# Weight sums of the first Strassen pair: read from the slots where they are made, or through DRAM

## The chip, the cores and the metric

One core of a Trainium2 chip. The metric is the device time of the kernel in microseconds (us), the median of three runs; a profile of one more execution stands beside it. Engines: PE (TensorE, matmuls), ACT (ScalarE), DVE (VectorE), POOL (GpSimd); all DMAs of the work spoken of here are issued by SP (SyncE), in order.

## The reference

Banded attention feeds a gated feed-forward layer; everything is float32.

```python
scores = scale * np.matmul(q, k.transpose(0, 1, 3, 2))      # 8 x 8 heads, 576 x 64 each
scores = np.where((rel >= 0) & (rel < 64), scores, -1000000000.0)
scores = scores - np.max(scores, axis=-1, keepdims=True)
attn = np.exp(scores)
attn = attn / (np.sum(attn, axis=-1, keepdims=True) + 1e-09)
out = np.matmul(attn, v)
...
x = np.ascontiguousarray(attn_out.transpose(0, 2, 1, 3)).reshape(B * S, H * D)   # 4608 x 512
gate = 1.0 / (1.0 + np.exp(-(x @ w_gate)))                   # 512 -> 1536
val = x @ w_val
return (gate * val @ w_out).astype(np.float32)               # 1536 -> 512
```

The weights arrive as 64-bit numbers and are brought to float32 on the chip.

## The kernel before

**Tiles.** The 4608 tokens are worked through in 12 tiles of 384. Attention of a tile gives x, transposed (`xf`); the feed-forward layer takes it up to 1536 hidden rows, in 12 blocks of 128, for the gate and for the value (m = 0, 1), and down again. A float32 matmul is done as three, with each operand split in a rounded part and the rest (`split`, L144: a CAST on ACT, L145, and a subtraction, L146).

**Strassen pairs.** Tiles 0 and 1 go up with plain products (L342). The ten others go up in five pairs, s = 1 to 5. For a pair, a block k (0 to 5) and an m, the blocks k and k + 6 for both tiles are made by seven products (`product`, L519, matmuls in L537, six of 128x384 each) in place of eight. Their weight sides are called A11, S2, S1, S3, A12, A22 and S4. The A parts are blocks of the weights; the S parts are sums and differences of these. A product's partial results are gathered in three PSUM banks per pair (pr0, pr1, pr2), with only one buffer each, and combined by DVE (u and c, L543). The first product of an m uses pr0 and so waits for all readers of pr0 of the m before; the fourth uses pr1 and waits for DVE's u.

**Where the weight parts lie.** All 14 parts of a k lie in DRAM, in seven tiles `wd[k][q]` of two parts (512 KB). The A parts are put there when the weights are converted (L140). The S parts are made once, for twelve (m, k): `sums_load` (L453) brings two float32 blocks back, `sums_make` (L464) makes four sums on POOL, `sums_split` (L474) splits them (CAST on ACT, subtraction on POOL) into two tiles `ws`, and `sums_store` (L482) writes these to `wd` in four DMAs. For each pair `w_load` (L440) loads the seven tiles of a k. The tiles `ws` and the loaded tiles `wt` take turns in one ring of seven slots (tag "W", WB = 7).

**Order.** A list of events with a planned time each (`put`) is sorted and gives the order in which instructions are handed to a scheduler; the engines run in that order. Into the pairs' stages are laid the pieces of attention for the pair after (scores and softmax L208, L230, L239; transposes L283, L288; outputs L312 with their copies `xf` on ACT, L267 to L271; normalise L249 to L252) and the down products (L407). In the stage s = 1 POOL has only the sums and their splits to do: normalise (L252) and the sums of x run on DVE there.

Of the kernel before, what the change touches and what calls it, by code (L numbers as in the profile page):

```python
# [9 lines left out]
F32 = mybir.dt.float32  # L10
F32R = mybir.dt.float32r
# [7 lines left out]
P = 128  # L19
# [7 lines left out]
def attn_ffn(ctx: ExitStack, tc: tile.TileContext, qT, kT, vN, w_gate, w_val, w_out, out):  # L27


    nc = tc.nc  # L30
    NTOK, DM = out.shape
# [11 lines left out]
    RAW, W32 = 6, 3  # L43

    const = ctx.enter_context(tc.tile_pool(name="const", bufs=1))
    wts = ctx.enter_context(tc.tile_pool(name="wts", bufs=1))
    xp = ctx.enter_context(tc.tile_pool(name="xp", bufs=1))
    mp = ctx.enter_context(tc.tile_pool(name="mp", bufs=2))
# [10 lines left out]
    for key in ((0, 0), (1, 0), (0, 1)):  # L59
        m = const.tile([P, P], F32, name=f"m_{key[0]}{key[1]}")  # L60
# [65 lines left out]
    def conv_c(i):  # L126
        j, m = divmod(i, KINDS)
        _, w32 = conv.pop(i)
        H = DM // 2
        tag, bufs = ("W", WB) if m < 2 else (f"wo_{j}", 1)  # L130
        w2 = wts.tile([P, 2, 2, H], F32R, name=f"w{m}_{j}", tag=tag, bufs=bufs)
        if m == 2:
# [19 lines left out]
    WB = 7  # L152
# [245 lines left out]
    def down(t, j, i, first, last):  # L398
# [9 lines left out]
        if last:  # L408
# [11 lines left out]
            else:  # L420
# [10 lines left out]
    PRODUCTS = [("A11", "B11", 0), ("S2", "T2", 1), ("S1", "T1", 2), ("S3", "T3", 1),  # L431
                ("A12", "B21", 0), ("A22", "T4", 1), ("S4", "B22", 2)]
    NPR = len(PRODUCTS)
    wd = [[dr.tile([P, 2, 2, DM // 2], F32, name=f"wd_{k}_{q}") for q in range(NPR)] for k in range(NK)]
    wt = {}
# [2 lines left out]
    hb = {}  # L438

    def w_load(s, k, q):  # L440
        wt[(s, k, q)] = wts.tile([P, 2, 2, DM // 2], F32R, name=f"wt_{s}_{k}_{q}", tag="W", bufs=WB)
        nc.sync.dma_start(out=wt[(s, k, q)].bitcast(F32), in_=wd[k][q])

    def put_part(m, k, name, parts):
        n = [w for w, _, _ in PRODUCTS].index(name)
# [1 line left out]
        nc.sync.dma_start(out=wd[k][q][:, half], in_=parts.bitcast(F32))  # L447


    EARLY = {(0, 0): 8, (1, 0): 10, (0, 1): 12, (1, 1): 8}  # L450
    sums = {}

    def sums_load(m, k):  # L453
        aa = []
        for i in range(2):
            if (m, k) in EARLY:
                a = xp.tile([P, DM], F32, name=f"a{i}_{m}_{k}", tag=f"x{EARLY[m, k] + i}")
            else:
                a = mp.tile([P, DM], F32, name=f"a{i}_{m}_{k}", tag="w32", bufs=W32)
            nc.sync.dma_start(out=a, in_=w32d[m][k + i * NK])  # L460
            aa.append(a)
        sums[m, k] = aa
# [9 lines left out]
        sums[m, k] = sw  # L472

    def sums_split(m, k):  # L474
        H = DM // 2
        sw, sums[m, k] = sums[m, k], []
        for i in range(0, 4, 2):
            w2 = wts.tile([P, 2, 2, H], F32R, name=f"ws{i}_{m}_{k}", tag="W", bufs=WB)
            split(sw[:, i:i + 2, :], w2[:, :, 0, :], w2[:, :, 1, :], nc.gpsimd)
            sums[m, k].append(w2)  # L480

    def sums_store(m, k):  # L482
        for i, w2 in enumerate(sums.pop((m, k))):
# [35 lines left out]
    def product(s, k, m, n):  # L519
        _, x, b = PRODUCTS[n]  # L520
        new = n in (0, 1, 2)
        if new:
            bk = psum(s, b, f"pr{b}_{m}_{s}_{k}")
            tmp[b] = bk[:, :TT]
            if n == 0:
                tmp["first"] = bk
        ps = tmp[b]
        q, half = divmod(NPR * m + n, 2)
        w2 = wt[(s, k, q)]
        prs = []  # L530
        for c in range(2):
            cs = slice(c * P, (c + 1) * P)
            whi, wlo = w2[:, half, 0, cs], w2[:, half, 1, cs]
            x2 = xs[(s, x, c)]
            prs += [(whi, x2[:, 0, :]), (whi, x2[:, 1, :]), (wlo, x2[:, 0, :])]
        for i, (l, r) in enumerate(prs):
            pe(nc.tensor.matmul(ps, l, r, start=new and i == 0, stop=i == len(prs) - 1,  # L537
                                skip_group_check=not new))
        nm = f"{m}_{s}_{k}"

        def plus(a, tag):
            o = mp.tile([P, TT], F32, name=f"{tag}{n}_{nm}", tag=tag, bufs=2)
            nc.vector.tensor_add(out=o, in0=ps, in1=a)  # L543
            return o

        if n == 0:
            tmp["p1"] = mp.tile([P, TT], F32, name=f"p1_{nm}", tag="p1", bufs=1)
            nc.scalar.copy(tmp["p1"], ps)  # L548
        elif n == 1:
            tmp["u2"] = plus(tmp["p1"], "u")  # L550
        elif n == 3:
            u3 = plus(tmp["p1"], "u")
            ps = tmp[2]
            result(s, k, m, 1, 1, plus(u3, "c"))
        elif n == 4:
            result(s, k, m, 0, 0, ps)
        elif n == 5:
            result(s, k, m, 1, 0, plus(tmp["p1"], "c"))
        elif n == 6:
            result(s, k, m, 0, 1, plus(tmp["u2"], "c"))  # L560
# [29 lines left out]
    def put(tm, o, f, *a):  # L590
        events.append((tm, o, f, a))
# [35 lines left out]
    at, now = {}, 0.0  # L627
# [14 lines left out]
    for i, (kind, t, j) in enumerate(plan):  # L642
        attend(i)
        at[(kind, t, j)] = now
        if (kind, t, j) == ("up", 0, 0):
            now = -9
# [12 lines left out]
        if (kind, t, j) == ("up", 0, 0):  # L659
            now = 0.0  # L660
    for i in range(KINDS * NF):
        j, m = divmod(i, KINDS)
# [29 lines left out]
    for s in range(1, NS):  # L692
        a, b = 2 * s, 2 * s + 1
        for c in range(2):
            put(now - 21 + 10 * c, 5, x_parts, s, c)
            for n in range(NPR):
                put(now - 19.5 + 10 * c + 1.2 * n, 5.5, x_part, s, n, c)
                put(now - 18 + 10 * c + 1.2 * n, 5.6, x_rest, s, n, c)
        downs = []
        fill.clear()  # L700
        if s + 1 < NS:

            for n, (i, d) in enumerate(((2, 7), (12, 9), (26, 5), (33, 9), (47, 5), (54, 9), (68, 5), (75, 5))):
                fill[i] = [(3, *unit(s + 1, n), *([unit(s + 1, n - 1)] if n else []))]
                fill[i + (2 if n else 4)] = [(4, *unit(s + 1, n))]
                fill[i + d] = [(1, *unit(s + 1, n))]
            fill[82] = [(2, *unit(s + 1, n))]
        slot = 0
        for k in range(NK):
            if s == 1:  # L710
                for m in range(2):
                    for d, f in ((-8, sums_load), (0, sums_make), (8, sums_split), (12, sums_store)):
                        put(now - 50 + 12 * m + d, 7, f, m, k)
            for q in range(NPR):
                put(now - (12 if s == 1 else 24) + 3 * q, 7.5, w_load, s, k, q)
            for m in range(2):
                for n in range(NPR):
                    put(now, 9, product, s, k, m, n)
                    now += PRT
                    if n in (2, 4, 6) and len(downs) > (RESERVE if m else 0) * (k == 1):  # L720
                        j, x = downs.pop(0)
                        put(now, 9, down, a, j, x, j == 0, False)
                        now += DPT
                    attend(slot)
                    slot += 1
            downs += [(j, x) for j in (k, k + NK) for x in range(TB)]
        for j, x in downs:
            put(now, 9, down, a, j, x, False, j == NF - 1)
            now += DPT
        last_tile(b, [n // 2 + (n % 2) * NK for n in range(NF)],  # L730
                        (4, lambda t, j, s=s: hidden_b(s, j)))
    events.sort(key=lambda x: (x[0], x[1]))
    for _, _, f, a in events:
        if f in (conv_a, conv_b, conv_c):
            with ExitStack() as behind:
                j, m = divmod(a[0], KINDS)
# [54 lines left out]
```

## Time and profile before

| | |
|---|---|
| median of three runs | 1011.78 us (1010.85 to 1012.56) |
| profiled execution, its own time | 1013.32 us |
| its span, first to last instruction | 1011.5 us |
| busy: PE, DVE, ACT, POOL | 97%, 67%, 52%, 23% |
| stage of pair s = 1 | 218.75 to 389.46 us |
| stages of s = 2 and s = 3 | 389.46 to 549.70, 549.70 to 710 us |
| loads wt<-wd, stores wd<-ws in all | 210 of 512 KB, 48 of 256 KB |

The span is shorter than the execution's own time by what lies before the first and behind the last instruction. A busy share is an average over all stages; what a single stage costs is read from windows and timelines of that stage. A timeline row gives start, duration, engine, line and tiles; a bracket behind it gives the idle time of the engine before it and what ended that.

### The profile page before, as it was taken

The page shows a single profiled execution, that of the slowest core. Times are in us where ns is not written, and L with a number is a line of the kernel's source. Part 1 is how long each engine was busy: PE and PEld are TensorE (multiplying, and loading weights), DVE is VectorE, ACT ScalarE, POOL GpSimd, SP SyncE. Part 2 cuts the span into 40 slices and gives each one's busy share as a digit, 9 for nine tenths or more (in the row PEclk, how much of TensorE's full clock was granted, in tenths as well). Part 3 has the DMA queues.
Part 4 walks back from the last instruction along what each step waited for, and adds up shares of the span by engine and source line. Part 5 has one row for each costly group of instructions (what it writes and reads, how often), then busy time and mean ns, then how long its engine had stood idle before and what let it go on. Part 6 is the DMA issues. An engine that isn't in the chain of part 4 may idle for free.

```text
span 1011.5 us, 19901 instructions
## 1 busy us (share of the span) xinstructions
PE 981.8 (97%) x6984; PEld 884.0 (87%) x6984; DVE 675.8 (67%) x1846; ACT 527.2 (52%) x1465; POOL 236.1 (23%) x251
## 2 busy tenths in 40 slices
PE   5899999998999999999999999999999999999998
PEld 4798998887899978999988999988999998999996
DVE  6789889757887874766675766675666677344542
ACT  7878886744654644545554654554555454211122
POOL 5200117254540030212131221213211124010100
PEclk9999999999999999999999999999999999999999
DMA  9899988899997624767652776760776662466500
GB/s 299 297 348 367 342 288 278 277 333 342 320 324 267 216 85 152 232 220 221 202 172 70 240 234 200 222 204 32 228 232 219 207 192 74 146 219 204 192 32 32
DMA packets 115924, 221.52 MB, mean 219 GB/s; under 512 B 9456, under 2 KB 61936, under 8 KB 115824
## 3 DMA queue, kind: packets, MB, share of 16 engines
q1 hardware_dynamic: 115824, 220.24, 65.9%
q8 instruction: 56, 0.92, 0.4%
q14 instruction: 44, 0.36, 0.1%
HBM read 178.52 MB, written 41.68 MB: 218 GB/s over the span
## 4 chain that ended last, share of the span: by engine, by line
PE 73%; DVE 7%; ACT 7%; DMA 6%; issue 3%; POOL 1%; SPq 0%; DVEq 0%; ACTq 0%; POOLq 0%
PE pr L537 36%; PE y L407 24%; PE ph L342 6%; ACT p L239 3%; PE pp L283 2%; PE s L208 2%; DMA wd<-w 2%; DMA wd<-ws 2%; ACT g L352 1%; ACT e L351 1%; PE oo L312 1%; PE s L312 1%; DMA wt<-wd 1%; DVE u L543 1%; DVE p L230 1%
## 5 line engine op out<-in xcount | busy, mean ns | idle before, releaser
L537 PE MATMUL pr<-x_T,wt 128*128 128x384 f32 x1440 | 284.6, 339 | 4.7 <-DVE u L543 3.6
L537 PEld LDWEIGHTS pr<-x_T,wt 128*128 128x128 f32 x1440 | 252.6, 188 | 20.1 <-DVE u L543 11.2
L407 PE MATMUL y<-w,hh 128*128 128x512 f32 x804 | 250.2, 392 | 0.0
L537 PE MATMUL pr<-x_B,wt 128*128 128x384 f32 x1080 | 222.2, 342 | 4.7 <-ACT xf L267 4.0
L537 PEld LDWEIGHTS pr<-x_B,wt 128*128 128x128 f32 x1080 | 188.7, 189 | 15.6 <-ACT xf L267 4.3
L407 PEld LDWEIGHTS y<-w,hh 128*128 128x128 f32 x804 | 148.3, 188 | 21.3 <-ACT hh L372 1.3
L543 DVE TENSOR_TENSOR u<-pr,p 128x384 f32<-128x384 f32 x120 | 66.6, 555 | 143.3 <-PE pr L537 143.0
L407 PE MATMUL y<-w,hl 128*128 128x512 f32 x402 | 158.6, 394 | 0.5 <-DVE hl L376 0.4
L252 POOL TENSOR_TENSOR p<-p,rs 128x384 f32<-128x384 f32 x76 | 65.0, 860 | 278.2 <-DVE rs L250 227.5
L239 ACT ACTIVATE p<-p,mn 128x128 f32<-128x128 f32 x288 | 111.1, 394 | 23.6 <-DVE mn L230 22.7
L376 POOL TENSOR_TENSOR hl<-h,hh 128x384 fp32r<-128x384 f32 x48 | 49.8, 1038 | 296.2 <-DVE hh L374 296.2
L342 PE MATMUL ph<-x,w 128*128 128x384 f32 x576 | 109.2, 343 | 1.8 <-DVE w L146 1.3
L342 PEld LDWEIGHTS ph<-x,w 128*128 128x128 f32 x576 | 100.9, 190 | 5.4 <-DVE w L146 1.6
L407 PEld LDWEIGHTS y<-w,hl 128*128 128x128 f32 x402 | 75.3, 187 | 19.3 <-DVE hl L376 3.1
L230 DVE CUSTOM_DVE_ANT_0 p<-s,m 128x128 f32<-128x128 f32 x288 | 66.4, 285 | 15.7 <-PE s L208 8.5
L543 DVE TENSOR_TENSOR c<-pr,u 128x384 f32<-128x384 f32 x120 | 66.6, 555 | 7.8 <-ACT g L568 3.3
L376 DVE TENSOR_TENSOR hl<-hb,hh 128x384 fp32r<-128x384 f32 x60 | 39.1, 663 | 40.9 <-ACT hh L372 40.5
L351 ACT ACTIVATE e<-c 128x384 f32<-128x384 f32 x72 | 37.4, 522 | 52.6 <-DVE c L543 51.6
L548 ACT COPY p<-pr 128x384 f32<-128x384 f32 x60 | 28.2, 470 | 70.4 <-PE pr L537 69.8
L288 ACT COPY pT<-pp 128x384 f32<-128x384 f32 x96 | 41.2, 481 | 41.6 <-PE pp L283 41.6
L356 DVE SCALAR_TENSOR_TENSOR g<-g,e 128x384 f32<-128x384 f32 x96 | 55.2, 589 | 5.7 <-ACT e L353 5.6
L354 DVE TENSOR_SCALAR g<-g 128x384 int32<-128x384 int32 x96 | 40.2, 425 | 25.9 <-ACT g L352 25.9
(84 smaller groups left out, 1238.7 us busy)
## 6 DMA issues: line engine op xcount, KB each, us to landing
wt<-wd SPq DMA_DIRECT2D x210, 512.0 KB, 4.2
v<-in_vN_dram SPq DMA_DIRECT2D x48, 384.0 KB, 4.9
wd<-ws SPq DMA_DIRECT2D x48, 256.0 KB, 5.3
k<-in_kT_dram SPq DMA_DIRECT2D x48, 224.0 KB, 5.0
q<-in_qT_dram SPq DMA_DIRECT2D x48, 192.0 KB, 4.7
wd<-w SPq DMA_DIRECT2D x36, 256.0 KB, 6.0
out_dram<-yo SPq DMA_DIRECT2D x33, 256.0 KB, 2.0
raw<-in_moe_w_gate_dram SPq DMA_DIRECT2D x12, 512.0 KB, 5.9
```

The costliest lines, as they stand in the source:

```text
L230: nc.vector.tensor_tensor_reduce(out=pt[:, u, :], in0=sc[:, u, :], in1=masks[key], op0=ALU.add, op1=ALU.min, scale=-SCALE, scalar=3.0e38, ...
L239: exp = nc.scalar.activation(pt[:, u, :], pt[:, u, :], AF.Exp, bias=mn[:, u:u + 1], scale=-1.0, **sums)
L252: eng.tensor_mul(out=pt, in0=pt, in1=rs.unsqueeze(2).broadcast_to([P, UP, P]))
L288: cp = nc.scalar.copy(pT, pp)
L342: pe(nc.tensor.matmul(ph, l, r, start=i == 0, stop=i == len(prs) - 1))
L351: nc.scalar.activation(e, ph, AF.Relu, scale=-1.0)
L354: nc.vector.tensor_scalar(out=g.bitcast(I32), in0=g.bitcast(I32), scalar1=0x7FFFFFFF, scalar2=None, op0=ALU.bitwise_and)
L356: nc.vector.scalar_tensor_tensor(out=g, in0=g, scalar=1.0, in1=e, op0=ALU.add, op1=ALU.mult)
L376: return eng.tensor_sub(out=h_lo, in0=h32, in1=h_hi.bitcast(F32))
L407: pe(nc.tensor.matmul(yb[y], l, r, start=first and n == 0, stop=last and n == 2))
L537: pe(nc.tensor.matmul(ps, l, r, start=new and i == 0, stop=i == len(prs) - 1, skip_group_check=not new))
L543: nc.vector.tensor_add(out=o, in0=ps, in1=a)
```

## The change

For the first pair, the products read the S parts from the tiles `ws` in which they were made; only the six A parts of a k are loaded (`a_load`: three tiles `wa`, two DMAs of 256 KB each). The stores stay, since the pairs after read all parts from DRAM. `wt` is now kept by part. The planned times of the sums are set anew: the sums of all k but 0 are made 21 before the k's first product, in place of 50, with a step of 13 between the two m, in place of 12, and of k = 0 by 38 before it. Two of the early sums get other tiles.

```diff
     def w_load(s, k, q):
-        wt[(s, k, q)] = wts.tile([P, 2, 2, DM // 2], F32R, name=f"wt_{s}_{k}_{q}", tag="W", bufs=WB)
-        nc.sync.dma_start(out=wt[(s, k, q)].bitcast(F32), in_=wd[k][q])
+        w2 = wts.tile([P, 2, 2, DM // 2], F32R, name=f"wt_{s}_{k}_{q}", tag="W", bufs=WB)
+        nc.sync.dma_start(out=w2.bitcast(F32), in_=wd[k][q])
+        for half in range(2):
+            wt[(s, k, *divmod(2 * q + half, NPR))] = w2[:, half]
+
+
+    OTHERS = [((0, 0), (0, 4)), ((0, 5), (1, 0)), ((1, 4), (1, 5))]
+
+    def a_load(s, k, x):
+        w2 = wts.tile([P, 2, 2, DM // 2], F32R, name=f"wa_{k}_{x}", tag="W", bufs=WB)
+        for i, (m, n) in enumerate(OTHERS[x]):
+            q, half = divmod(NPR * m + n, 2)
+            nc.sync.dma_start(out=w2[:, i].bitcast(F32), in_=wd[k][q][:, half])
+            wt[(s, k, m, n)] = w2[:, i]
...
-    EARLY = {(0, 0): 8, (1, 0): 10, (0, 1): 12, (1, 1): 8}
+    EARLY = {(0, 0): 8, (1, 0): 10}
...
+            elif (m, k) == (0, 1):
+                if i == 0:
+                    both = mp.tile([P, 2, DM], F32, name=f"a_{m}_{k}", tag="raw", bufs=RAW)
+                a = both[:, i, :]
...
             sums[m, k].append(w2)
+            for e in range(2):
+                n = [w for w, _, _ in PRODUCTS].index(f"S{i + e + 1}")
+                wt[(1, k, m, n)] = w2[:, e]
...
-        q, half = divmod(NPR * m + n, 2)
-        w2 = wt[(s, k, q)]
+        w2 = wt[(s, k, m, n)]
...
-            whi, wlo = w2[:, half, 0, cs], w2[:, half, 1, cs]
+            whi, wlo = w2[:, 0, cs], w2[:, 1, cs]
...
-                    for d, f in ((-8, sums_load), (0, sums_make), (8, sums_split), (12, sums_store)):
-                        put(now - 50 + 12 * m + d, 7, f, m, k)
-            for q in range(NPR):
-                put(now - (12 if s == 1 else 24) + 3 * q, 7.5, w_load, s, k, q)
+                    for d, f in ((-6, sums_load), (0, sums_make), (7, sums_split), (11, sums_store)):
+                        put(now - (21 if k else 38) + 13 * m + d, 7, f, m, k)
+                for x, d in enumerate((-18, -14, -5)):
+                    put(now + d, 7.5, a_load, s, k, x)
+            else:
+                for q in range(NPR):
+                    put(now - 24 + 3 * q, 7.5, w_load, s, k, q)
```

The change alters the order on ACT, SP and POOL. On ACT, at the end of the first k and the start of the second of s = 1, before the change (ws0_0_3 is the first tile of sums of m = 0, k = 3, xf_4_0 a piece of x of tile 4, p0_4_2 a piece of its softmax, pr0_1_1_0 the bank pr0 for m = 1, s = 1, k = 0):

```order
L353 ACTIVATE e_3_0_3243<-e_3_0_3243 128x384
L288 COPY pT0_4_0_3301<-pp0_4_0_3297 128x128
L288 COPY pT1_4_0_3307<-pp1_4_0_3303 128x128
L145 CAST ws0_0_3_3403<-sw_0_3_3255 128x2x256
L145 CAST ws2_0_3_3406<-sw_0_3_3255 128x2x256
L267 COPY xf_4_0_3369<-pr0_1_1_0_3266 128x128
L268 COPY xf_4_0_3369<-s1_4_2_3356 128x128
L239 ACTIVATE p0_4_2_3384,rs0_4_2_3386<-p0_4_2_3384,mn0_4_2_3385 128x128 x3
L271 COPY xf_4_0_3369<-s0_4_2_3355 128x128
L239 ACTIVATE p1_4_2_3394,rs1_4_2_3396<-p1_4_2_3394,mn1_4_2_3395 128x128 x3
L548 COPY p1_0_1_1_3427<-pr0_0_1_1_3420 128x384
```

The same place of ACT after the change:

```order
L353 ACTIVATE e_3_0_3183<-e_3_0_3183 128x384
L288 COPY pT0_4_0_3244<-pp0_4_0_3240 128x128
L288 COPY pT1_4_0_3250<-pp1_4_0_3246 128x128
L145 CAST ws0_1_1_3355<-sw_1_1_3224 128x2x256
L267 COPY xf_4_0_3307<-pr0_1_1_0_3206 128x128
L268 COPY xf_4_0_3307<-s1_4_2_3294 128x128
L239 ACTIVATE p0_4_2_3322,rs0_4_2_3324<-p0_4_2_3322,mn0_4_2_3323 128x128 x3
L271 COPY xf_4_0_3307<-s0_4_2_3293 128x128
L145 CAST ws2_1_1_3358<-sw_1_1_3224 128x2x256
L239 ACTIVATE p1_4_2_3332,rs1_4_2_3334<-p1_4_2_3332,mn1_4_2_3333 128x128 x3
L567 COPY p1_0_1_1_3368<-pr0_0_1_1_3361 128x384
L145 CAST ws0_0_2_3433<-sw_0_2_3341 128x2x256
```

Before, both CASTs of the sums of m = 0, k = 3 stood ahead of the first xf copy, three k ahead of their use. Now one CAST of m = 1, k = 1 stands there, the second behind the xf copies, and the first of m = 0, k = 2 ahead of the gate activations of k = 1.

On SP, around the start of the stage, before the change (yo are output rows, a0 and a1 the two blocks of `sums_load`, wt the loads of weight parts):

```order
L422 DMA out_0_dram<-yo_1_0_3077 128x512
L442 DMA wt_1_0_6_3209<-wd_0_6_168 128x1024
L422 DMA out_0_dram<-yo_1_1_3091 128x512
L422 DMA out_0_dram<-yo_1_2_3102 128x512
L442 DMA wt_1_1_0_3211<-wd_1_0_169 128x1024
L460 DMA a0_0_3_3125<-w32d_0_3_140 128x512
L167 DMA q_4_2_3249<-in_qT_dram 128x384
L460 DMA a1_0_3_3127<-w32d_0_9_146 128x512
L168 DMA k_4_2_3250<-in_kT_dram 128x448
```

SP around the same place after the change (wa are the loads of `a_load`):

```order
L422 DMA out_0_dram<-yo_1_0_3026 128x512
L422 DMA out_0_dram<-yo_1_1_3043 128x512
L476 DMA a0_1_1_3123<-w32d_1_1_150 128x512
L422 DMA out_0_dram<-yo_1_2_3054 128x512
L476 DMA a1_1_1_3125<-w32d_1_7_156 128x512
L476 DMA a0_0_2_3229<-w32d_0_2_139 128x512
L453 DMA wa_1_0_3066<-wd_1_0_169 128x512
L453 DMA wa_1_0_3066<-wd_1_2_171 128x512
L167 DMA q_4_2_3190<-in_qT_dram 128x384
L168 DMA k_4_2_3191<-in_kT_dram 128x448
```

The blocks for the sums of m = 1, k = 1 are now loaded between and behind the output stores of tile 1, where before the blocks of m = 0, k = 3 were; the loads of weight parts are half as large.

## Rows read from the trace of the kernel before

**Rows 1.** The page's span and busy time of each engine.

```profile
span 1011.5 us, 19901 instructions
PE 981.8 (97%) x6984; PEld 884.0 (87%) x6984; DVE 675.8 (67%) x1846; ACT 527.2 (52%) x1465; POOL 236.1 (23%) x251
```

**Rows 2.** Windows: us, busy PE, PEld, DVE, ACT, POOL; PE clock, DMA share, GB/s.

```profile
218.75:300.00 81.25, 73.70 (x570) 67.50 (x569) 63.16 (x170) 44.11 (x136) 38.21 (x39) 0.98 0.96 330
240.00:260.00 20.00, 17.90 (x93) 17.36 (x93) 13.20 (x37) 11.08 (x34) 6.90 (x7) 0.91 0.91 332
...
218.75:389.46 170.71, 162.62 (x1154) 145.15 (x1153) 124.45 (x326) 88.88 (x265) 49.31 (x48) 0.99 0.74 250
389.46:549.70 160.24, 159.61 (x1153) 143.92 (x1153) 105.32 (x298) 81.97 (x250) 35.15 (x36) 1.00 0.59 189
```

**Rows 3.** Timeline of PE, 218 to 300 us.

```profile
219.82 2.24 PE L537 MATMUL pr<-x_T,wt 128*128 128x384 f32 x12
...
227.84 1.33 PE L537 MATMUL pr<-x_B,wt 128*128 128x384 f32 x6 [0.57 <-ACT g L352]
...
242.10 2.29 PE L537 MATMUL pr<-x_B,wt 128*128 128x384 f32 x6 [4.03 <-ACT xf L267]
244.18 2.80 PE L537 MATMUL pr<-x_T,wt 128*128 128x384 f32 x12
...
248.58 1.20 PE L537 MATMUL pr<-x_B,wt 128*128 128x384 f32 x6
...
253.12 1.23 PE L537 MATMUL pr<-x_B,wt 128*128 128x384 f32 x6
...
266.02 1.31 PE L537 MATMUL pr<-x_T,wt 128*128 128x384 f32 x6 [0.81 <-DVE c L543]
...
269.69 1.32 PE L537 MATMUL pr<-x_T,wt 128*128 128x384 f32 x6 [1.66 <-DVE u L543]
...
282.14 1.31 PE L537 MATMUL pr<-x_T,wt 128*128 128x384 f32 x6 [0.23 <-DVE u L543]
...
292.75 1.32 PE L537 MATMUL pr<-x_T,wt 128*128 128x384 f32 x6 [0.25 <-DVE u L543]
```

**Rows 4.** Timeline of ACT, 241 to 265 us.

```profile
241.26 0.62 ACT L145 CAST ws<-sw 128x512 fp32r<-128x512 f32 x1 [6.54 <-DMA wd<-ws]
241.78 0.26 ACT L267 COPY xf<-pr 128x128 f32<-128x128 f32 x1
...
263.96 0.62 ACT L145 CAST ws<-sw 128x512 fp32r<-128x512 f32 x1 [2.59 <-DMA wd<-ws]
```

**Rows 5.** The chain that ended last, 218 to 300 us: start, us, what.

```profile
234.86 6.30 DMA wd<-ws
```

**Rows 6.** Timeline of DVE, 266 to 270 us.

```profile
266.69 1.67 DVE L252 TENSOR_TENSOR p<-p,rs 128x384 f32<-128x384 f32 x1
...
269.09 0.54 DVE L543 TENSOR_TENSOR u<-pr,p 128x384 f32<-128x384 f32 x1
```

**Rows 7.** Timeline of POOL, 257 to 267 us.

```profile
257.63 1.06 POOL L468 TENSOR_TENSOR sw<-a 128x256 f32<-128x256 f32 x1
258.66 0.73 POOL L470 TENSOR_TENSOR sw<-a,a 128x256 f32<-128x256 f32 x1
...
266.65 1.29 POOL L146 TENSOR_TENSOR ws<-sw,ws 128x512 fp32r<-128x512 f32 x1 [0.71 <-ACT ws L145]
```

**Rows 8.** By line (ns min/median/max): L252 to 300 us, L252 after, L352 in both.

```profile
L252 DVE TENSOR_TENSOR p<-p,rs x8: 548/558/1674, 225.5 to 280.8; 128x384 f32<-128x384 f32 x8
...
L252 DVE TENSOR_TENSOR p<-p,rs x6: 549/550/560, 301.5 to 336.7; 128x384 f32<-128x384 f32 x6
...
L352 ACT ACTIVATE g<-c x18: 507/518/527, 226.5 to 348.0; 128x384 f32<-128x384 f32 x18
```

**Rows 9.** DMA issues 218 to 345 us (KB, us to landing); SP's waits, 150 to 400.

```profile
wt<-wd SPq DMA_DIRECT2D x40, 512.0 KB, 5.4
...
SPq L442 <- PE pr L537: 47.0, 28, 3.1
```

## The prediction

> **What bounds the kernel now.** The page is read first: TensorE (PE) is busy for 981.8 of a span of 1011.5 us, 97% [rows 1], so a change can give back only time in which PE waits or runs slowly, and the question is whether such time lies in the stage that the change touches. The busy time by windows answers it. A stage of a Strassen pair that has nothing to do with the weight sums, the second, lasts 160.24 us, and PE works for 159.61 of them. The first pair's stage, which makes the sums, lasts 170.71 us, with PE busy for 162.62 [rows 2]. So the first pair costs 10.5 us more than its successor, of which 8.1 us is idle and the rest is slower matmuls. Those 10.5 us are the most that this change can give.
>
> The timeline of PE then shows where they lie [rows 3]. Idle: 0.57 us before 227.84, behind ScalarE's (ACT's) gate activation; 4.03 us before 242.10, behind ACT's copy xf; 0.81 us before 266.02, behind a VectorE (DVE) addition c; 1.66, 0.23 and 0.25 us before 269.69, 282.14 and 292.75, behind DVE's u. Slow: the six matmuls at 242.10 take 2.29 us where six at 227.84 take 1.33, and the twelve at 244.18 take 2.80 where twelve at 219.82 take 2.24, which makes 0.96 + 0.56 = 1.52 us. The granted clock of 240 to 260 is 0.91 of full, a spell at 1.2 GHz within a stretch at 2.4, where other rows have about 1 [rows 2]; before it fell PE had been idle for the 4.03 us. So the slow matmuls are a second bill for the same wait.
>
> What ended the 4.03 us is read on ACT [rows 4]: a CAST of a weight sum (L145) stood at the head of ACT's queue for 6.54 us and was let go by a DMA wd<-ws, a store; the xf copy for which PE waited came right behind it, at 241.78. The chain shows that store as its longest piece there, 6.30 us from 234.86 [rows 5]. The CAST needs one of the seven W slots, and the slot is free only when the sum that lay in it has been written out to DRAM. The 0.81 us has the same source one step later: another CAST waited 2.59 us for such a store until 263.96 [rows 4], the score copies behind it came late, and with them DVE's pieces of softmax, which stand ahead of c.
>
> The 1.66 us is of another kind. A DVE normalise (L252) took 1.67 us, from 266.69, and the u that PE needed came only at 269.09 [rows 6]; GpSimd (POOL) had begun a split (1.29 us) at 266.65 [rows 7]. Of eight such normalises up to 300 us the median is 558 ns and the longest 1674; of six after 300 us, where POOL has next to no work, none is longer than 560 [rows 8].
>
> **What the change does, in pieces.** (1) The sums' parts stay in the slots in which they were made, until their product. ACT's CASTs of the next k therefore no longer wait for a store but for a matmul that is done at about that time: the order of instructions puts one CAST before the xf copy where two stood, and its slot comes free with the last but one product before that copy. I take the 4.03, the 1.52 and the 0.81 us as gone: 6.36 us. The bounds of this piece are nothing (if the CAST at this place waits as long for something else) and 6.36.
>
> (2) The read-back shrinks from 42 loads of 512 KB to 36 of 256 KB, 22.0 MB to 9.4. No PE wait in rows 3 ends on a load, so I cost this at nothing; the load takes 5.4 us [rows 9] and the new loads are issued as soon as their slot is free, twelve or more products ahead of use (a half of k, seven products, took 11.0 us, from 242.10 to 253.12 [rows 3]). Without that cover a load would cost up to 5.4 us at each k. SyncE's queue waited 47.0 us in 28 waits for PE's slots already [rows 9]; the new loads wait on PE too, and the q, k and v loads of the pair after stand behind them as they stood behind the old ones: also nothing.
>
> (3) The CASTs are queued elsewhere on ACT. For every k one now stands ahead of the gate activations that free PSUM bank pr0 for the next half. That chain is one CAST (0.62 us [rows 4]) and four activations of about 0.52 us [rows 8], 2.7 us, and PE needs the bank only two products and two sets of down matmuls after the product that starts the chain: 253.12 less the end of the product at 248.58, 3.3 us [rows 3]. So nothing, and up to 0.6 us at each of five k if the cover is gone. The first k has no down matmuls between; its 0.57 us stays.
>
> (4) The sums move later. In the order of POOL, 20 splits and 9 sums now lie in the first pair's stage, before it 15 and 6. A sum is four additions of 0.7 to 1.1 us and a split 1.29 [rows 7], so 3 x 3.3 + 5 x 1.3 = 16.4 us of POOL work join the 38.2 us of 218.75 to 300 [rows 2]. There the collisions with DVE have cost 1.66 + 0.23 + 0.25 = 2.14 us, so at the same rate the new work costs 16.4 / 38.2 x 2.14 = 0.9 us. No row shows what it costs at the new places. Its low bound is -2.14 (the collisions vanish as well), its high bound is a full 1.66 at each of the eight score steps of this stage, 13.3 - 2.14 = 11.1 us. I take 0.9 and one more full collision, 2.6 us: nearer to the rate, since in rows 3 only one wait of DVE out of four had full size, and above it, since POOL is now busy at all k and the first k has no slack.
>
> A rule bears on (4) and speaks against the change. By the Trainium skill, page "SBUF — State Buffer", section "SBUF: two separate sides", GpSimd and a DVE operation with two SBUF inputs share a port pair by an exclusive lock, and the one that comes second is blocked for the whole instruction of the first. The 1674 ns of L252 beside 558 agrees with it. By the rule alone DVE pays for every overlap; what that would make of the time here, if PE paid with it, is the slower rival below.
>
> **Sum.** -6.36 + 2.6 = -3.8 us. The profiled execution took 1013.32 us with a span of 1011.5; by the sum its span becomes 1007.7. That execution lies 1.54 us above the median of the three runs shown, 1011.78, so against the median the forecast is 1008.0 us.
>
> **Rivals.** *Full gain, no new collisions* (chance 0.20): POOL's work falls between DVE's operations, as it did from 276 to 300, where it was busy and PE lost 0.48 us in two waits [rows 3]. Then 1011.8 - 6.4 = 1005.4 us, and 1003.3 if the old collisions go too. Against it: POOL has more to do at the same boundaries.
>
> *The wait only changes its name* (0.18, within 0.2%): the CAST ahead of xf needs the sum as well as the slot, and that sum is now made from a load that stands in SyncE's queue behind the output stores of tile 1. If it is four us late, ACT blocks there as before, the 4.03 and 1.52 stay, only 0.81 is won and 2.6 lost: 1013.6. Those stores are issued at the start of the stage, 218.75 [rows 2]; if they hold the load up by 2 us, 5.4 for the load [rows 9] and 3.3 for the sum bring it to about 230. The bank that xf is copied from is filled shortly before PE stops, at 238.07, and the CAST's slot comes free one product earlier, at about 236, so some six us of slack speak against it. A partial form, with half of the wait, ends near 1011.
>
> *Phase-locked collisions, slower* (0.12): the splits are now let go by PE's products, so they come at a fixed point of each k, right behind its last product, where DVE's softmax and normalise for the next score step stand. If each of the eight steps pays 1.66, the added cost is 11.1 and the result 1011.8 - 6.4 + 11.1 = 1016.5 us. It turns the sign from four full hits more than before (6.36 / 1.66). Against it: at 282.14 and 292.75 POOL worked around the same boundary and PE lost a quarter of a us.
>
> **How the numbers follow.** The forecast has 0.50, with a range of its own of 1006 to 1010: the cost of (4) between 0.5 and 4.2. A measurement here can tell about 0.2%, 2.0 us, from no change, that is, faster means under 1009.8. Forecast and full gain are faster, 0.70; the renamed wait is the same, 0.18; the phase-locked case slower, 0.12. The range goes from 1004.4 (most of the full gain) to 1012.4 (most of the renamed wait); about 0.06 is left out below and 0.14 above.
>
> **What would show it.** Right: no ACT wait on wd<-ws in the first pair's stage; no PE idle time of over 1 us at the first boundary between two k; no stretch there with a lower clock; a stage of about 167 us in place of 170.7; the second stage still 160.2. For (4): waits of PE for DVE's u or c of 0.2 to 1.7 us, now also after 300, each beside a DVE operation on SBUF that is two or three times as long as its median, with a POOL instruction beside it. Wrong: an ACT CAST that waits for POOL's sum or for PE for over 2 us, a load wa on which PE waits, or collisions that add up to over 6 us.

## The result, and the profile after

The changed kernel takes 1016.53 us (median of 20 runs, 1014.6 to 1020.38), the kernel before 1012.79 us (20 runs, 1010.85 to 1016.88). The ratio is 1.0033, 95% interval 1.0021 to 1.0044: 3.7 us slower. The forecast was 1008.0 us with a range of 1004.4 to 1012.4; the "phase-locked" rival had 1016.5.

The page of the profiled execution (1014.76 us by its own time) reads almost as [rows 1]:

```profile
span 1013.0 us, 19884 instructions
PE 980.7 (97%) x6984; PEld 883.9 (87%) x6984; DVE 680.2 (67%) x1846; ACT 528.2 (52%) x1465; POOL 237.4 (23%) x251
```

Windows, to be read beside [rows 2] (us, then busy time of PE, PEld, DVE, ACT, POOL; PE clock, DMA share, GB/s):

```profile
216.06:300.00 83.94, 74.02 (x569) 67.27 (x568) 68.50 (x164) 44.68 (x134) 43.53 (x41) 0.98 0.74 239
280.00:300.00 20.00, 18.76 (x133) 17.48 (x134) 14.11 (x29) 7.14 (x18) 8.87 (x9) 0.91 0.65 209
216.06:390.73 174.67, 162.69 (x1153) 145.09 (x1152) 134.99 (x326) 92.61 (x270) 70.21 (x64) 0.99 0.63 201
390.73:550.73 160.00, 159.37 (x1153) 143.74 (x1152) 105.32 (x298) 81.97 (x250) 35.18 (x36) 1.00 0.60 190
```

The first pair's stage, from its first product to that of the second pair, lasts 174.67 us. The same two products start at 218.75 and 389.29 us in the trace before, 170.54 us apart. The 4.1 us more lie in this stage alone; the second is as long as ever. (The stage starts 2.7 us earlier here; over the fourteen profiles of this study its start lies between 215.4 and 218.8 without regard to the kernel, so that is not the change's.) PE's busy time is that of before, so the loss is idle time. POOL and DVE are both busy for longer: 70.2 against 49.3 us and 135.0 against 124.5.

The timeline of PE, which answers to [rows 3] (lines after 440 have moved by about 20: L562 is the old L543, L556 the old L537):

```profile
225.15 1.31 PE L556 MATMUL pr<-x_B,wa 128*128 128x384 f32 x6 [0.57 <-ACT g L352]
...
231.74 1.31 PE L556 MATMUL pr<-x_T,ws 128*128 128x384 f32 x6 [2.46 <-DVE u L562]
...
240.99 1.33 PE L556 MATMUL pr<-x_T,ws 128*128 128x384 f32 x6 [0.85 <-DVE c L562]
...
244.50 1.31 PE L556 MATMUL pr<-x_T,ws 128*128 128x384 f32 x6 [1.48 <-DVE u L562]
...
263.31 1.32 PE L556 MATMUL pr<-x_T,ws 128*128 128x384 f32 x6 [0.90 <-DVE c L562]
...
266.82 1.32 PE L556 MATMUL pr<-x_T,ws 128*128 128x384 f32 x6 [1.49 <-DVE u L562]
...
281.24 1.56 PE L556 MATMUL pr<-x_T,ws 128*128 128x384 f32 x6 [2.17 <-DVE u L562]
282.60 2.12 PE L556 MATMUL pr<-x_B,wa 128*128 128x384 f32 x6
...
306.70 1.32 PE L556 MATMUL pr<-x_T,ws 128*128 128x384 f32 x6 [2.06 <-DVE u L562]
```

The 4.03 us behind ACT's xf copy are gone, and seven waits for DVE have come: 11.41 us in all, against 2.95 before. After the one at 281.24 the next matmuls are slow, 2.12 us for six where 1.20 is usual; the window 280 to 300 has a granted clock of 0.91. What DVE and POOL did ahead of three of these waits shows why. First DVE, then POOL, 240 to 245 us:

```profile
240.39 0.55 DVE L562 TENSOR_TENSOR c<-pr,u 128x384 f32<-128x384 f32 x1
...
241.72 1.45 DVE L252 TENSOR_TENSOR p<-p,rs 128x384 f32<-128x384 f32 x1
243.09 0.68 DVE L249 TENSOR_SCALAR rs<-rs 128x3 f32<-128x3 f32 x1
...
243.90 0.55 DVE L562 TENSOR_TENSOR u<-pr,p 128x384 f32<-128x384 f32 x1
```

```profile
241.07 1.68 POOL L146 TENSOR_TENSOR ws<-sw,ws 128x512 fp32r<-128x512 f32 x1
242.72 1.03 POOL L487 TENSOR_TENSOR sw<-a,sw 128x256 f32<-128x256 f32 x1
```

Normalise takes 1.45 us beside POOL's split, and the next short operation 0.68 beside POOL's sum; u can only follow. The same happens to the gate's steps ahead of 231.74, where POOL worked without a gap until 230.53 (two splits from 224.95, then additions). DVE after, then the last four of these steps in the trace before, where POOL was idle from 227.2 to 230.5:

```profile
225.33 1.45 DVE L354 TENSOR_SCALAR g<-g 128x384 int32<-128x384 int32 x1
...
227.17 0.97 DVE L354 TENSOR_SCALAR g<-g 128x384 int32<-128x384 int32 x1
228.07 1.09 DVE L356 SCALAR_TENSOR_TENSOR g<-g,e 128x384 f32<-128x384 f32 x1
229.08 0.88 DVE L354 TENSOR_SCALAR g<-g 128x384 int32<-128x384 int32 x1
229.88 1.07 DVE L356 SCALAR_TENSOR_TENSOR g<-g,e 128x384 f32<-128x384 f32 x1
```

```profile
228.68 0.35 DVE L354 TENSOR_SCALAR g<-g 128x384 int32<-128x384 int32 x1
228.94 0.55 DVE L356 SCALAR_TENSOR_TENSOR g<-g,e 128x384 f32<-128x384 f32 x1
229.41 0.36 DVE L354 TENSOR_SCALAR g<-g 128x384 int32<-128x384 int32 x1
229.68 0.55 DVE L356 SCALAR_TENSOR_TENSOR g<-g,e 128x384 f32<-128x384 f32 x1
```

The third place is the score step ahead of 281.24. Normalise on DVE, then the split on POOL, after the change:

```profile
276.60 1.62 DVE L252 TENSOR_TENSOR p<-p,rs 128x384 f32<-128x384 f32 x1
```

```profile
276.52 1.29 POOL L146 TENSOR_TENSOR ws<-sw,ws 128x512 fp32r<-128x512 f32 x1 [3.60 <-ACT ws L145]
```

The same two in the trace before:

```profile
279.91 0.56 DVE L252 TENSOR_TENSOR p<-p,rs 128x384 f32<-128x384 f32 x1
```

```profile
276.79 1.29 POOL L146 TENSOR_TENSOR ws<-sw,ws 128x512 fp32r<-128x512 f32 x1 [5.28 <-ACT ws L145]
```

Before, the split is over long before normalise, and PE loses 0.23 us at that place; after, it begins 0.08 us ahead of it, and PE loses 2.17 us. The wait of 2.06 us at 306.70 has the same picture: a split from 301.97 and a normalise of 1.69 us from 301.99. Added up from the records of the first 145 us of the stage, DVE's operations take some 12 us more than the medians of their kinds before the change and some 24 us after it.

### The profile page after: what moved, and what is told of

The parts are those of the page before. It is cut to its first block, busy times and chain, and to the rows that moved or that the text cites. A ratio compares the mean times of both kernels' runs of the same rounds, so it can differ in the third digit from the quotient of the medians.

```text
span 1013.0 us, 19884 instructions
## 1 busy us (share of the span) xinstructions
PE 980.7 (97%) x6984; PEld 883.9 (87%) x6984; DVE 680.2 (67%) x1846; ACT 528.2 (52%) x1465; POOL 237.4 (23%) x251
## 4 chain that ended last, share of the span: by engine, by line
PE 72%; DVE 9%; ACT 8%; issue 4%; DMA 4%; POOL 1%; SPq 0%; DVEq 0%; POOLq 0%; ACTq 0%
PE pr L556 34%; PE y L407 25%; PE ph L342 5%; ACT p L239 3%; PE pp L283 2%; PE s L208 2%; ACT g L352 1%; DMA wd<-w 1%; PE oo L312 1%; ACT e L351 1%; DVE u L562 1%; DVE c L562 1%; DVE p L230 1%; PE s L312 1%; DMA v<-in_vN_dram 1%
## 5 line engine op out<-in xcount | busy, mean ns | idle before, releaser
L556 PE MATMUL pr<-x_T,wt 128*128 128x384 f32 x1152 | 226.8, 339 | 1.7 <-DVE u L562 1.5
L556 PEld LDWEIGHTS pr<-x_T,wt 128*128 128x128 f32 x1152 | 201.6, 188 | 13.5 <-DVE u L562 7.3
L556 PE MATMUL pr<-x_B,wt 128*128 128x384 f32 x864 | 176.6, 340 | 0.2
L562 DVE TENSOR_TENSOR u<-pr,p 128x384 f32<-128x384 f32 x120 | 66.6, 555 | 145.5 <-PE pr L556 145.3
L556 PEld LDWEIGHTS pr<-x_B,wt 128*128 128x128 f32 x864 | 150.6, 188 | 8.2 <-issue 2.6
L252 POOL TENSOR_TENSOR p<-p,rs 128x384 f32<-128x384 f32 x76 | 64.6, 854 | 278.2 <-DVE rs L250 242.3
L562 DVE TENSOR_TENSOR c<-pr,u 128x384 f32<-128x384 f32 x120 | 66.5, 555 | 7.8 <-ACT g L587 3.3
L354 DVE TENSOR_SCALAR g<-g 128x384 int32<-128x384 int32 x96 | 47.2, 499 | 27.1 <-ACT g L352 27.1
L567 ACT COPY p<-pr 128x384 f32<-128x384 f32 x60 | 28.1, 469 | 70.6 <-PE pr L556 70.2
L372 ACT CAST hh<-hb 128x384 fp32r<-128x384 f32 x60 | 30.0, 512 | 51.6 <-PE y L407 51.5
```

The costliest lines, as they stand in the source:

```text
L252: eng.tensor_mul(out=pt, in0=pt, in1=rs.unsqueeze(2).broadcast_to([P, UP, P]))
L354: nc.vector.tensor_scalar(out=g.bitcast(I32), in0=g.bitcast(I32), scalar1=0x7FFFFFFF, scalar2=None, op0=ALU.bitwise_and)
L372: nc.scalar.copy(h_hi, h32)
```

## The experiments

Theory 1: POOL's work on the sums holds DVE's operations up, and PE waits for DVE. Theory 2, the rival: DVE's own queue is too long where its instructions now stand, whatever POOL does. A second question is what reading from the slots is worth by itself. The kernel before runs beside each group of four: 1012.77, 1013.67 and 1013.52 us (medians of 23, 23 and 24 runs). "Stage" is the time from the first product of the first pair to that of the second, in the profiled execution; "DVE waits" is the sum of PE's idle times there behind c and u. Each version has one profile. Those of e5 and e9 are of the fastest of their executions, 3.7 and 3.2 us below their medians; the others lie within 2 us of theirs.

| | us | ratio to before, 95% | stage | DVE waits |
|---|---|---|---|---|
| before | 1012.8 | | 170.5 | 2.95 |
| after | 1016.5 | 1.0021 to 1.0044 | 174.7 | 11.41 |
| e1 after, POOL memset | 1001.9 | 0.9868 to 0.9913 | 163.5 | 2.11 |
| e2 before, POOL memset | 1004.1 | 0.9881 to 0.9931 | 163.2 | 1.59 |
| e3 after, normalise on POOL | 1011.1 | 0.9961 to 0.9992 | 170.9 | 6.65 |
| e4 after, normalise a slot later | 1016.3 | 1.0021 to 1.0051 | 173.7 | 10.43 |
| e5 before, normalise on POOL | 1012.5 | 0.9972 to 1.0007 | 169.3 | 5.02 |
| e6 after, splits on DVE | 1007.4 | 0.9923 to 0.9956 | 167.2 | 4.95 |
| e7 after, sums shifted | 1008.2 | 0.9931 to 0.9967 | 167.3 | 6.11 |
| e8 after, e3 and e7 together | 1011.0 | 0.9960 to 0.9985 | 169.8 | 5.53 |
| e9 before, splits on DVE | 1010.3 | 0.9944 to 0.9983 | 167.7 | 3.39 |
| e10 after, e6 and e7 together | 1007.9 | 0.9917 to 0.9969 | 167.8 | 4.70 |
| e11 after, sums 3 later | 1008.5 | 0.9926 to 0.9964 | 167.0 | 5.99 |
| e12 after, sums 3 earlier | 1015.9 | 1.0004 to 1.0036 | 174.3 | 10.87 |

**e1 and e2: POOL reads next to nothing**, in the kernel after and before. The additions and the subtraction work on 8 of 256 columns and memset fills the rest, so both kernels leave the weight sums out of the result.

```diff
+    T = 8
...
+        if cols:
+            eng.memset(lo[:, :, cols:].bitcast(F32), 0.0)
+            w32, hi, lo = w32[:, :, :cols], hi[:, :, :cols], lo[:, :, :cols]
         eng.tensor_sub(out=lo, in0=w32, in1=hi.bitcast(F32))
...
-        nc.gpsimd.tensor_add(out=sw[:, 0, :], in0=a2[:, :H], in1=a2[:, H:])
+        nc.gpsimd.tensor_add(out=sw[:, 0, :T], in0=a2[:, :T], in1=a2[:, H:H + T])
...
+        nc.gpsimd.memset(sw[:, :, T:], 0.0)
...
-            split(sw[:, i:i + 2, :], w2[:, :, 0, :], w2[:, :, 1, :], nc.gpsimd)
+            split(sw[:, i:i + 2, :], w2[:, :, 0, :], w2[:, :, 1, :], nc.gpsimd, T)
```

> The changed kernel, in which POOL's sums and splits read next to nothing: the four additions and the subtraction work on 8 columns, and the rest of their outputs is set to zero by memset, so the weight sums are left out of the result. Number and order of the steps stay. Theory 1 (POOL's reads hold DVE up): in the first pair's stage the waits of PE for DVE's u and c, 0.85 to 2.46 us each and 11.4 us in all in the changed kernel, go, and with them the slow matmuls after 280 us; L252 is never above 0.6 us; the stage falls from 174.7 to 161 to 163 us and the time from 1016.5 to 1003 to 1006 us. Theory 2 (DVE's own queue is too long where its instructions now stand, whatever POOL does): the waits stay within a few tenths and the time is 1014 to 1018 us.

> The kernel before, with the same replacement on POOL (the weight sums are left out of the result). Theory 1: only the waits for u at 269.69, 282.14 and 292.75 go, 2.1 us, and perhaps part of the 0.81; the ACT CAST that waits for a store keeps PE waiting by 3 to 4 us with its slow matmuls, so the time is 1009 to 1011.5 us, 4 to 7 us above the changed kernel with the same replacement; that difference is what reading from the slots is worth by itself. If the store wait was itself made by POOL's slowness, the 4 us go too, the time falls to 1004 to 1006, and the two kernels end within 2 us of each other.

Measured: 1001.9 and 1004.1 us, stages of 163.5 and 163.2. In e1 normalise (now L257) is never held up:

```profile
L257 DVE TENSOR_TENSOR p<-p,rs x16: 548/558/591, 223.5 to 339.2; 128x384 f32<-128x384 f32 x16
```

Of the 11.41 us 2.11 are left, at two places (1.23 at 272.52, 0.88 at 295.27), and the time falls by 14.6 us by the medians, 1.1 below what theory 1 gave; between the two profiled executions it is 11.3 us, and the stage is 11.2 us shorter. Theory 1 stands: DVE's queue holds the same operations, only POOL's work is lighter. That it is both lighter to read and shorter (the memsets take 0.53 us where the splits took 1.3 to 1.7) is not separated by this pair. e2 went the second way that was expected of it: the kernel before gains 8.6 us, not 2 to 3. ACT's copy xf, for which PE had waited 4.03 us, comes in time, though the CAST ahead of it still waits for a store. ACT in e2 (L147 is the CAST, L272 the copy), then PE:

```profile
235.47 0.62 ACT L147 CAST ws<-sw 128x512 fp32r<-128x512 f32 x1 [2.04 <-DMA wd<-ws]
236.01 0.26 ACT L272 COPY xf<-pr 128x128 f32<-128x128 f32 x1
```

```profile
235.37 2.37 PE L543 MATMUL pr<-x_B,wt 128*128 128x384 f32 x12
```

With [rows 4] beside it: 2.04 us of waiting in place of 6.54, and twelve matmuls of two products without a break between. So in this profile the store wait no longer reaches PE once POOL is light: the store can leave only when POOL has made the split. How much of the 4.03 us changes from one execution to the next was not measured. With POOL light, the stages of the two kernels are equal within 0.3 us, and the medians differ by 2.2 us, with intervals of the two ratios that overlap: reading from the slots by itself is worth 2.2 us by the medians and nothing by the stages.

**e3 and e5: normalise of tiles 4 and 5 on POOL**, after and before.

```diff
-        eng = nc.vector if t == 3 and p % 2 or t // 2 == 2 else nc.gpsimd
+        eng = nc.vector if t == 3 and p % 2 else nc.gpsimd
```

> The changed kernel, with normalise (L252) of tiles 4 and 5 on POOL in place of DVE, as in the later pairs. Theory 1: the operation that is held up longest leaves DVE, u follows c after two short operations, and the waits for u shrink to 0 to 0.8 us each: 1007 to 1011 us. Theory 2: DVE saves the unhindered 0.55 us twice per boundary, at most 3 to 4 us in all: 1012.5 to 1014 us. A wait that could take their place: transposes of softmax (PE pp) that wait for POOL, which has a split or a sum ahead of normalise; then PE idles before L283 by 1 us or more and the time stays above 1013.

> The kernel before, with normalise of tiles 4 and 5 on POOL. In it only one normalise was held up at a cost to PE (1.66 us); the store wait of 4 us and its slow matmuls are not touched. Theory 1: 1010 to 1012 us, and the changed kernel with the same edit (1011.1) no longer stands behind the kernel before, because what the change lost was lost in those operations. If POOL, now with more to do, makes its splits and so the stores later, ACT's wait grows and the time is 1013 to 1017.

Measured: 1011.1 and 1012.5 us, the upper end of theory 1's range and half a us above it. The changed kernel gains 5.4 us, more than the 3 to 4 of theory 2, with no operation less in all; the waits for u at the boundaries between two k shrink from 1.48 and 1.49 us to 0.48 each, two ahead of which the gate's steps stand stay (1.95 at 232.49, 1.73 at 281.05). PE does not wait for transposes in e3; in e5 it does once, for 0.55 us. In e5 the wait for xf is 0.30 us, not 4.03, which the edit does not explain. The profile is of e5's fastest execution, so this may be a difference between executions; it was not tried. With normalise off DVE the two kernels stand within 1.4 us of each other.

**e4: the normalise step planned one product later.**

```diff
-                fill[i + (2 if n else 4)] = [(4, *unit(s + 1, n))]
+                fill[i + (2 if n else 4) + (s == 1)] = [(4, *unit(s + 1, n))]
```

> The changed kernel, with the normalise step of tiles 4 and 5 planned one product later. POOL's work is untouched. Theory 1: L252 is held up as before (maximum still 1.4 to 1.7 us), but in four or more of the eight places it stands behind u, not ahead of it, and PE waits less there: 1009 to 1013 us. If the wait then hits the next operation in DVE's queue (the c of the fourth product, or the gate's steps) the time stays at 1014 to 1017.

Measured: 1016.3 us. This run tells nothing of the theories: in the trace of the stage DVE's operations, and POOL's, stand in the same order as without the edit. It is a second measurement of the changed kernel, and its waits for u are the same ones (1.50, 1.51, 2.20 and 2.06 us from the first boundary on) but for the first, 1.38 us in place of 2.46. So the sum of the DVE waits is good to about 1 us from one profile to another.

**e6 and e9: the splits' subtraction on DVE**, after and before.

```diff
-            split(sw[:, i:i + 2, :], w2[:, :, 0, :], w2[:, :, 1, :], nc.gpsimd)
+            split(sw[:, i:i + 2, :], w2[:, :, 0, :], w2[:, :, 1, :], nc.vector)
```

> The changed kernel, with the subtraction of the 24 splits on DVE in place of POOL: DVE gets about 0.7 us for each of 20 in the first pair's stage, 14 us more, and POOL loses 30 of its 59 us. Theory 1: the holds by splits (L252 of 1.4 to 1.7 us) go, those by sums stay; PE's waits for DVE fall from 11.4 to 4 to 7 us and the time to 1009 to 1013. Theory 2 (DVE's queue is too long): 14 us more work in that queue make the waits longer: 1018 to 1026.

> The kernel before, with the subtraction of the splits on DVE, as e6 did with the changed kernel (1007.4). Theory 1: POOL is no longer late for the stores, so ACT's wait for a store shrinks to under 1 us as in e2, and the holds of L252 by splits go: 1006 to 1009 us, within 2 us of e6, so that the change itself is worth next to nothing once POOL is out of the way. If the store wait has a cause of its own (the number of DMAs, SyncE's queue), it stays, and the time is 1010.5 to 1014.

Measured: 1007.4 and 1010.3 us. e6 ends 1.6 us below the range of theory 1. This decides against theory 2: DVE has 20 operations more in the stage, 13.7 us, and PE waits for it 4.95 us in place of 11.41. By line in e6 (ns, shortest/median/longest):

```profile
L252 DVE TENSOR_TENSOR p<-p,rs x16: 546/558/843, 223.0 to 342.4; 128x384 f32<-128x384 f32 x16
...
L146 DVE TENSOR_TENSOR ws<-sw,ws x20: 674/686/992, 224.7 to 330.0; 128x512 fp32r<-128x512 f32 x20
```

The subtraction takes 0.69 us on DVE, half of what it takes on POOL, and normalise is held by the sums alone, to 0.84 us. e9 ends 3 us above e6, outside what I expected (within 2), though the intervals of the two ratios overlap: the CAST ahead of xf waits 4.27 us for a store there and PE 1.53 us for xf. So a store wait is left in the kernel before with the splits off POOL. That it is smaller than 4.03 us in a usual execution is not shown, since this profile is of e9's fastest.

**e7, e11 and e12: the sums at another place in the plan.** e7 shifts them by five, with a step of 11 and later splits of m = 1; e11 and e12 change one number, 21 to 18 and to 24. The edit of e7:

```diff
-                    for d, f in ((-6, sums_load), (0, sums_make), (7, sums_split), (11, sums_store)):
-                        put(now - (21 if k else 38) + 13 * m + d, 7, f, m, k)
+                    sp = (3, 8)[m] if k else 7
+                    for d, f in ((-6, sums_load), (0, sums_make), (sp, sums_split), (sp + 4, sums_store)):
+                        put(now - (16 if k else 38) + (11 if k else 13) * m + d, 7, f, m, k)
```

> The changed kernel, with the sums planned five later (16 before the first product of their k, step 11) and the splits of m = 1 put behind the boundary. The work of each engine is the same; only its place in a k moves. Theory 1 with the addition that the place decides: PE's waits for DVE change in place and size by several us in all, to between 3 and 8 us, and the time is 1006 to 1013. If POOL's amount of work decides and not its place, the waits stay at 10 to 13 us and the time at 1014.5 to 1018.

> The changed kernel, with only the base of the sums' plan moved, to 18 before the first product in place of 21. Some neighbours on DVE change places, as in e7. If the place of POOL's work in a k decides: a time between those of the changed kernel and e7, 1008 to 1015. If what helped in e7 was the step of 11 and the later splits of m = 1: 1015 to 1018.

> The changed kernel, with the base of the sums' plan at 24 before the first product in place of 21. DVE's order is that of the changed kernel but for one pair of neighbours; POOL's order changes. If only DVE's order made e7 faster: 1015.5 to 1018 us, as the changed kernel. If POOL's place decides: different by 2 us or more, either way, with the waits for u at other sizes.

Measured: 1008.2, 1008.5 and 1015.9 us. No work is added or taken away, and three units of plan, later, give back 8 us. What differs in e11 is seen at the place of the 2.46 us wait. POOL begins its two splits 10.3 us into the stage there, in place of 8.9, with the additions behind them and not ahead. The gate's steps, which stand at the same time of the stage as in the changed kernel, have their usual length but one. DVE, then POOL:

```profile
226.43 0.35 DVE L354 TENSOR_SCALAR g<-g 128x384 int32<-128x384 int32 x1
226.69 0.55 DVE L356 SCALAR_TENSOR_TENSOR g<-g,e 128x384 f32<-128x384 f32 x1
227.16 0.36 DVE L354 TENSOR_SCALAR g<-g 128x384 int32<-128x384 int32 x1
227.43 0.56 DVE L356 SCALAR_TENSOR_TENSOR g<-g,e 128x384 f32<-128x384 f32 x1
227.90 1.46 DVE L354 TENSOR_SCALAR g<-g 128x384 int32<-128x384 int32 x1
229.28 0.54 DVE L562 TENSOR_TENSOR u<-pr,p 128x384 f32<-128x384 f32 x1
```

```profile
227.52 2.98 POOL L146 TENSOR_TENSOR ws<-sw,ws 128x512 fp32r<-128x512 f32 x2 [13.84 <-ACT ws L145]
```

Neither this wait nor the 0.57 us ahead of it is found in e11's timeline; at the second boundary, where a split still lies beside normalise (1.45 us), the waits of 0.90 and 1.50 are the same as after. At the place of the 2.17 us wait, normalise is not held in e11 (0.56 us at 274.29) and the wait is 0.76. One reservation: in e7 and e11 some neighbours on DVE have changed places too, for example u ahead of a reciprocal of 0.17 us, and what that adds was not tried apart.

e12 ended where it was expected to if only DVE's order made e7 faster, but it does not show that. In its trace POOL does the same operations in the same order as in the changed kernel, at the same distance to DVE's to within some tenths of a us, and normalise is held at the same places (1.44, 1.45, 1.62 and 1.70 us). The edit moved neither, so e12 is a third measurement of the changed kernel. What three units earlier would do, had POOL's work moved, no run shows.

**e8 and e10: two edits together.** e8 has those of e3 and e7, e10 those of e6 and e7.

> The changed kernel with both edits: normalise of tiles 4 and 5 on POOL, and the sums planned five later with the splits of m = 1 behind the boundary. If both act on the same waits, it ends at 1007 to 1010 us, below each alone and below the kernel before. If the shift puts POOL's work ahead of normalise, PE waits for softmax's transposes instead and it ends above 1011.

> The changed kernel, with the splits on DVE (e6, 1007.4) and the sums shifted as in e7 (1008.2). The waits that each leaves are 4 to 5 us. If the shift keeps the sums' additions away from the score steps: 1003 to 1006 us. If the shift helped only through the splits: 1006 to 1009.

Measured: 1011.0 and 1007.9 us, e8 between its two cases and e10 in its second. The edits do not add up. In e8 a wait of 2.30 us for u has come at 254.09, and PE also waits 0.92 us for a transpose behind normalise on POOL. e10 is no faster than e6. Of the versions that compute all, e6 is the fastest, 0.6% under the kernel before and 0.9% under the changed one, with e7, e10 and e11 less than 1.2 us behind it.

## Why the prediction was wrong

**What bounds it, and the place.** Right: all that changed lies in the first pair's stage, and the second is untouched.

**(1), the store wait.** The mechanism was right, the size was not a price of its own. ACT no longer waits for a store; its waits in front of a CAST, from 205 to 345 us in the trace after the change, are these (us in all, times, longest), and no store is among them:

```profile
ACT ws L145 <- issue: 22.4, 5, 7.8
ACT ws L145 <- POOL sw L487: 4.3, 1, 4.3
ACT ws L145 <- POOL sw L485: 4.2, 1, 4.2
ACT ws L145 <- PE pr L556: 2.8, 2, 2.3
```

The 4.03 us are gone as said, and so are the slow matmuls at that place. The 0.81 us were not won: for the same c PE now waits 0.90 us, at 263.31, with DVE busy without a gap from an operation of 1.52 us (L594 at 258.72) beside a split of 1.65. And the 6.36 us were booked as the worth of reading from the slots, while in e2 a lighter POOL takes the 4.03 and the 1.52 away without it. Where POOL is lighter in both kernels, the medians differ by 2.2 us (e1 against e2) and 3.0 us (e6 against e9), the stages by 0.3 us the other way and by 0.5 us. The CASTs that wait 4.3 and 4.2 us for POOL's sum, and the one that waits 2.3 for PE, were a sign of being wrong in the prediction; no PE wait ends on them.

**(2) and (3).** Right at nothing: no PE wait ends on a load wa, and the wait for the gate activation is 0.57 us as before.

**(4), the sums moved later: the step that failed.** It was sized at 2.6 us; PE's waits for DVE rose from 2.95 to 11.41, by 8.5 us. The slow matmuls, which I had booked as gone, came back behind the 2.17 us wait: 0.25 + 0.92 + 0.50 = 1.67 us (the rows of 281.24 and 282.60, and down matmuls of 1.05 and 0.48 us where 0.63 and 0.40 are usual) in place of 1.52. Together -4.03 + 8.46 + 0.15 = 4.6 us, of which the stage shows 4.1.

The mistake was to carry a rate, 2.14 us of waiting for 38.2 us of POOL's work, to places where POOL had not worked before, with one full collision on top. By place the 8.46 us are these:

| place, after the change | DVE waits before | after | what differs |
|---|---|---|---|
| 231.74 | none | 2.46 | POOL was idle there before, waiting for a block of weights |
| 240.99, 244.50 | none | 0.85, 1.48 | PE was waiting for xf there before; the split now lies on normalise |
| 263.31, 266.82 | 0.81, 1.66 | 0.90, 1.49 | about the same |
| 281.24 | 0.23 | 2.17 | the split now lies on normalise |
| 306.70 | none | 2.06 | the split now lies on normalise |
| 292.75 in the trace before | 0.25 | none | |

Only the 0.85 us are a collision that a larger wait had covered: at that boundary POOL was busy before the change too and DVE was held up (L575 took 1.52 us from 237.42), but PE was waiting for xf from 238.07 and paid nothing more. The normalise behind it was not held (0.55 us at 244.79). The rest, 2.46, 1.48, 1.94 and 2.06 us, are new meetings. Nor was 1.66 us the most that a place can cost, since several operations in a row are held ahead of u: three of the seven waits are longer. POOL was busy for 20.9 us more in the stage, where 16.4 were counted.

So four of the eight score steps pay, and the gate's steps of the first k, which were not counted, pay most. The "phase-locked" rival had the kind of thing right, splits that fall on normalise, with 13.3 us where 11.41 were measured. That its 1016.5 us is the measured time is luck in part: it let all eight steps pay 1.66 us each, and it counted the 6.36 us as gone without the slow matmuls' return and without the 0.90.

**The rule of the Trainium skill** that part (4) cites (page "SBUF — State Buffer", section "SBUF: two separate sides") pointed the right way, slower, and the rows agree that the one that begins second waits: the normalise at 276.60, 0.08 us behind a split, took 1.62 us, and one at 316.30, 0.05 us ahead of a split, took 0.55 us while the split took 1.68. So DVE does not pay for every overlap, as the prediction read the rule, and what PE pays had to come from the places.

## What to carry to other kernels

A wait that is removed may have been covering something: before its price is booked, look at what the other engines do in that very interval and let them pay. A rate of contention holds for the places where it was measured. When work moves, lay its new times beside the operations that stand ahead of what PE waits for: the same split cost 0.23 us when it was over before normalise and 2.17 us when it began 0.08 us ahead of it. Three units of plan were worth 8 us here (with a few neighbours on DVE exchanged), and moving the splits onto the engine that they held up was worth 9.

## What the runs showed of the hardware

DVE's u and c, which read PSUM (L543 before, L562 after), took 523 to 560 ns in all fourteen profiles, whatever POOL did; the c at 226.70 after the change took 0.55 us in the middle of two splits (224.95 to 227.93). Operations on SBUF alone took up to 1.7 us. Which engine was held went by the order in which they began. To set beside the pair at 276.60 and 276.52 above, DVE, then POOL, later in the same trace:

```profile
316.30 0.55 DVE L252 TENSOR_TENSOR p<-p,rs 128x384 f32<-128x384 f32 x1
```

```profile
316.35 1.68 POOL L146 TENSOR_TENSOR ws<-sw,ws 128x512 fp32r<-128x512 f32 x1 [2.52 <-ACT ws L145]
```

In e1, where POOL wrote with memset, normalise with its two SBUF inputs was not held (591 ns at most; two of the sixteen began inside a memset, 0.3 and 0.5 us before its end), but the little L249 (L254 there), with one, was: 1.54 us beside two memsets. DVE, then POOL, in e1:

```profile
269.39 1.54 DVE L254 TENSOR_SCALAR rs<-rs 128x3 f32<-128x3 f32 x1 [0.62 <-ACT p L244]
```

```profile
269.12 1.78 POOL L493 MEMSET sw<- 128x992 f32 x2
```

The Trainium skill, page "SBUF — State Buffer", section "SBUF: two separate sides", says that a DVE operation with two SBUF inputs is blocked only by a GpSimd operation that reads SBUF, and one in a 2-port perf mode by any. That normalise was not held beside memset agrees, as far as two cases go; that L249 runs in such a mode no run here shows.

The clock did not follow from the length of a wait alone: the matmuls behind 2.17 us of idle time at 281.24 were slow (granted clock 0.66 of full from 281 to 286, a spell at 1.2 GHz), those behind 2.46 us at 231.74 were not (1.31 us for six, a clock of 1.00 until 240). In e12 the same wait, 2.44 us, was followed by slow ones: 2.05 and 1.96 us for six, with a clock of 0.83 from 234 to 244.
